# A planner that prices array forms by kind, corner products for K's tail, and six PSUM banks for attention

## The chip, the cores and the metric

The kernel runs on one core of one Trainium2 chip. The metric is the time of one execution in device microseconds. TensorE (PE) multiplies, VectorE (DVE) and ScalarE (ACT) do the elementwise work and read the results out of PSUM, SyncE (SP) issues the DMAs, and GpSimd (POOL) only sets up constants. PSUM has eight banks of 128 partitions x 512 f32.

## The reference

Two stages, one feeding the other. First linear attention over 8 batches x 8 heads, 576 tokens, head size 64, with 128 features:

```python
def phi(x):
    proj = np.einsum('bhsd,df->bhsf', x, w_phi)
    proj = proj - np.max(np.abs(proj), axis=-1, keepdims=True)
    return np.concatenate([np.exp(proj), np.exp(-proj)], axis=-1)
q_p, k_p = (phi(q), phi(k))
kv = np.einsum('bhsf,bhsd->bhfd', k_p, v)
z = np.sum(k_p, axis=2)
num = np.einsum('bhsf,bhfd->bhsd', q_p, kv)
den = np.einsum('bhsf,bhf->bhs', q_p, z)[..., None] + 1e-06
out = num / den
```

Then a gated feed-forward over the 4608 tokens (x is 4608 x 512, the inner width 1536):

```python
gate = 1.0 / (1.0 + np.exp(-(x @ w_gate)))
val = x @ w_val
y = gate * val @ w_out
```

All in f32. Attention's products run on TensorE as f32. The feed-forward's run as three fp32r products each (high x high, high x low, low x high), so each weight and each activation is held as a high and a low part (`wh`/`wl`, `xh`/`xl`, `hh`/`hl`).

## The kernel before

**Attention** goes in 32 steps, one for each batch and pair of heads. In the program's tile names a step is: `pk`, the projection of K (`keys`: eight products on 64x128 halves of the array, then one 128x128 product for the last 64 tokens of both heads, laid out in `kin` as a block diagonal, into the third bank `pk_2`); `pq`, the projection of Q in two halves of 288 tokens; `px`, a product that spreads Q's maxima (steps 0 to 9 only); `kvz`, K's features times V and their sums, in four 128x32 strips; `tp`, three 128x128 transposes of the result; `nm`, the numerator, and `dp`, the denominator, both in strips. Between them, DVE takes maxima and subtracts (`mx`, `dk`, `pm`, `mb`, `d`), and ACT takes exponentials and copies out of PSUM (`ek`, `eq`, `d`, `kvt`, `kv`, `ex`, `dr`).

**Feed-forward** takes the tokens in nine chunks of 512 and the inner width in twelve blocks j of 128. Pass A does j = 0 to 3 for all chunks while attention is still running: for each chunk and j one unit, which is 12 matmuls into a bank `gA` and 12 into a bank `vA`; ACT takes a tanh and an exponential of `gA` (`tA`, `uA`), DVE makes the gate and multiplies it with `vA` (line 812: it frees `vA`'s bank), and `hhA`/`hlA` come out. After the four units of a chunk, four `acc` groups of 12 matmuls multiply with w_out, and the half result goes to HBM (`ys`). Pass B does j = 4 to 11 in the same way with names ending in B, once the weights of these j are there. The weights have to be split into high and low parts, eight instructions for each of 36 pieces (`wraw`, `wtop`, `wmid`, `wh`, `wl`). The pieces of j = 4 to 11 are prepared after all of attention is done, since they take its SBUF.

**The order of the work** is made when the program is built. Each operation is handed to `Plan` with an engine, a cost, what it follows, the buffers it takes, a rank and (on PE) a `mode`. `Plan.run` then walks through time: of the operations that can start first it takes the lowest rank, on PE with the discount `STICK` for one of the mode that PE is already in, and 0.15 us added to the cost of one of another mode. The modes are "row" (`pk`, `pq`), "strip" (`kvz`, `nm`, `dp`) and "full" (`px`, `tp` and the whole feed-forward). The order so made is the fixed order of instructions on each engine; on the chip each engine goes through its own in order and waits for semaphores.

**PSUM banks** are handed out by the planner as well: attention after the first steps takes them from `shared` (banks 0 to 4), pass A of the feed-forward from `apart` (banks 5 to 7), pass B from all eight.

Of the kernel before, what the change touches and what calls it, by code (L numbers as in the profile page):

```python
# [19 lines left out]
B, H, S, D = 8, 8, 576, 64  # L20
F = 128
P = 128
# [11 lines left out]
JA = 4  # L34
SOON = (3,)
PERM = 10
ONPE = 10
STICK = 0.3
GATE = -1.0
EXN = 2  # L40
HN = 5
# [27 lines left out]
class Op:  # L69
    def __init__(self, eng, cost, fn, after, uses, takes, rank, mode, lag):  # L70
        self.eng, self.cost, self.fn, self.rank, self.mode = eng, cost, fn, rank, mode
        self.after, self.takes, self.lag, self.end = after, takes, lag, None
        self.left, self.then = 0, []
        for b in (*uses, *takes):
            b.users.append(self)


LAG = {"PE": 0.27, "DVE": 0.13, "ACT": 0.2, "SP": 2.0, "POOL": 0.2, None: 0.0}
# [2 lines left out]
class Plan:  # L81
# [14 lines left out]
    def run(self, trace=None):  # L96
        free, mode = collections.defaultdict(float), None
        for op in self.ops:
            op.left = len(op.after)
            for a in op.after:  # L100
                a.then.append(op)
        ready = [op for op in self.ops if not op.left]
        n = 0
        while ready:
            best = {}
            for op in ready:
                t = free[op.eng]
                for a in op.after:
                    t = max(t, a.end - (a.lag if a.eng == op.eng == "PE" else 0.0))
                op.at, taken = [], set()  # L110
                for b in op.takes:
                    u, k = b.place(taken)
                    t = max(t, u)
                    taken.add((id(b.slots), k))
                    op.at.append(k)
                if t < 1e9:
                    best.setdefault(op.eng, []).append((t, op))
            if not best:
                raise RuntimeError("no operation can start")
            eng = min(best, key=lambda e: min(t for t, _ in best[e]))  # L120
            t0 = min(t for t, _ in best[eng])

            def rank(c):
                t, op = c
                return op.rank - (STICK if op.mode and op.mode == mode else 0.0), t

            t, op = min((c for c in best[eng] if c[0] <= t0 + 0.05), key=rank)
            ready.remove(op)
            cost = op.cost
            if eng == "PE":  # L130
                cost += 0.15 if op.mode != mode else 0.0
                mode = op.mode
            if trace is not None:
                trace.append((t, cost, op))
            free[eng] = t + cost
            op.end = t + cost + op.lag
            if eng == "SP" and op.mode:
                self.wire = max(self.wire, t) + op.mode / 240.0
                op.end = max(op.end, self.wire + op.lag)
            for b, k in zip(op.takes, op.at):  # L140
                b.slots.held[k], b.n = b, k
            op.fn()
            n += 1
            for o in op.then:
                o.left -= 1
                if not o.left:
                    ready.append(o)
        assert n == len(self.ops)
# [11 lines left out]
def attention_moe(  # L160
# [10 lines left out]
    nc = tc.nc  # L171
    vec, act, pool = nc.vector, nc.scalar, nc.gpsimd
    ctx.enter_context(tc.manual_schedule())
    plan = Plan()
# [9 lines left out]
    at = right.enter_context(tc.tile_pool(name="at", bufs=2, side="right"))  # L184
    ps = ctx.enter_context(tc.tile_pool(name="ps", bufs=1, space=PSUM))
    banks = Slots(8)
    alone, shared, apart = range(8), range(5), range(5, 8)
    homes = {"wp": wp1, "ws": at}

    def bank(b, shape, name):  # L190
# [25 lines left out]
    wk = at1.tile([P, F], F32, name="wk")  # L216
# [11 lines left out]
    def head(hd):  # L228
        return slice(hd * D, hd * D + D)
# [102 lines left out]
    def attention(i):  # L332
# [22 lines left out]
        def keys():  # L355
            for g, pk in enumerate(pks):
                bank(pk, [P, 4, F], f"pk{n}_{g}")
            kx = T["kin"]
            for t in range(4):
                for hd in range(2):  # L360
                    nc.tensor.matmul(  # L361
                        pks[hd].t[:, t, :], kx[head(hd), t * P : t * P + P],
                        wk[head(hd), :], start=True, stop=True,
                    )
            nc.tensor.matmul(
                pks[2].t[:, 0, :], kx[:, 4 * P :], wk, start=True, stop=True
            )

        ko = plan("PE", 1.2, keys, [lk], [kin], pks, rank=i - 0.6, mode="row")
        mx, dk = buf("mx", 2), buf("dk", 1)  # L370
        eks = []

# [80 lines left out]
        qc = []  # L453
        for hf in range(2):
            pqs = [Buf(banks, mine) for _ in range(2)]
            qo = plan("PE", 0.6, q_half(hf, pqs), [lq, ko], [qin], pqs, rank=i - 0.5, mode="row")
            qc.append(
                plan(
                    "ACT", 2 * act_time(HS), q_copy(hf, pqs), [qo, *qc],
                    [*pqs, *([d] if hf else [])], [] if hf else [d], rank=i - 0.4,  # L460
                )
            )
# [68 lines left out]
        def kv():  # L531
# [25 lines left out]
                    )  # L557

        kvo = plan(
            "PE", 3.2 if onpe else 2.6, kv, [ke, lv, *ksum], [ek, vin, *su], [kvz],  # L560
            rank=i, mode="strip",
        )
        kvt, kvb = buf("kvt", 1), buf("kv", 2)
# [33 lines left out]
                            start=sg == 0, stop=sg == 1, tile_position=(0, o),  # L597
                        )

        no = plan("PE", 2.0, num, [qf, kd], [eq, d, kvb], nms, rank=i, mode="strip")  # L600

        def num_copy():
            T["ex"] = at.tile([P, S], F32, tag="ex", name="ex" + n, bufs=EXN)
# [6 lines left out]
        def den():  # L610
# [12 lines left out]
                        )  # L623

        do = plan(
            "PE", 1.0 + soon, den, [no], [eq, d, kvb], dps, rank=i - 0.05, mode="strip"
        )
        rb = buf("rb", 1)
        if soon:
# [136 lines left out]
                acc, a[:, ts], w[:, ws], start=first and i == 0, stop=last and i == 2  # L766
            )

    hs, hdone = {}, {}
    MM = 0.2276  # L770

    def unit(S_, C, j, rank):
        key = (S_, C)
        n = f"{S_}{C}_{j}"
        T = {}
        gb, vb = (Buf(banks, apart if S_ == "A" else alone) for _ in range(2))
        tb, ub, hb = buf("t", 1), buf("u", 2), buf("h", HN)
        hs[C, j] = hb

        def gv(m, b):  # L780
            def go():
                bank(b, [P, CW], "gv"[m] + n)
                mm_in(b.t, xs[key], j, m)

            return go

        g = plan(
            "PE", 12 * MM, gv(0, gb), [*xdone[key], *wdone[j, 0]], [xbuf[key]], [gb],
            rank=rank, mode="full",
        )  # L790
        link("unit", g)
        vo = plan(
            "PE", 12 * MM, gv(1, vb), [g, *wdone[j, 1]], [xbuf[key]], [vb],
            rank=rank, mode="full",
        )
        link("unit", vo)

        def tanh():
            T["t"] = moe.tile([P, CW], F32, tag="t", name="t" + n, bufs=1)
            act.activation(T["t"], gb.t, AF.Tanh, scale=0.5)  # L800

        def exp():
            T["u"] = moe.tile([P, CW], F32, tag="u", name="u" + n)
            act.activation(T["u"], gb.t, AF.Exp)

        def absolute():
            tu = T["t"].bitcast(U32)
            vec.tensor_scalar(tu, tu, 0x7FFFFFFF, None, op0=ALU.bitwise_and)  # L808

        def times():  # L810
            t = T["t"]
            vec.scalar_tensor_tensor(t, t, 1.0, vb.t, op0=ALU.add, op1=ALU.mult)  # L812

        def gate():
            u = T["u"]
            vec.scalar_tensor_tensor(u, u, 1.0, T["t"], op0=ALU.min, op1=ALU.mult)  # L816

        def high():
            T["h"] = tuple(
                moe.tile([P, CW], F32R, tag=x, name=x + n, bufs=HN) for x in ("hh", "hl")  # L820
            )
            hb.t = T["h"]
            act.copy(T["h"][0], T["u"])  # L823

        def rest():
            hh, hl = T["h"]
            vec.tensor_tensor(hl, T["u"], hh.bitcast(F32), op=ALU.subtract)  # L827

        r = GATE
        o = plan("ACT", act_time(CW), tanh, [g], [gb], [tb], rank=r)  # L830
        e = plan("ACT", act_time(CW), exp, [g], [gb], [ub], rank=r)
        o = plan("DVE", vec_time(CW, True), absolute, [o], [tb], rank=r)
        o = plan("DVE", vec_time(CW), times, [o, vo], [tb, vb], rank=r)
        o = plan("DVE", vec_time(CW), gate, [o, e], [tb, ub], rank=r)
        o = link("high", plan("ACT", act_time(CW), high, [o], [ub], [hb], rank=r))
        hdone[C, j] = plan("DVE", vec_time(CW), rest, [o], [ub, hb], rank=r)
        return vo
# [28 lines left out]
    for C in range(NCK):  # L866
# [5 lines left out]
        for t in range(CW // P):  # L872
# [12 lines left out]
            def store(C=C, t=t, T=T):  # L885
# [2 lines left out]
            o = plan(  # L888
                "PE", 3 * JA * MM, accumulate,
                [*(hdone[C, j] for j in range(JA)), *(w for j in range(JA) for w in wdone[j, 2])],  # L890
                [hs[C, j] for j in range(JA)], [ab], rank=100 + 10 * C + 15, mode="full",
            )
            outs.append(o)
            o = plan("ACT", act_time(DM) + 0.08, half, [o], [ab], [yb], rank=GATE)
            ydone[C].append(plan("SP", 0.06, store, [o], [yb], rank=90, mode=256))
# [9 lines left out]
    for C in range(NCK):  # L905
# [3 lines left out]
        for j in js:  # L909
# [3 lines left out]
            for t in range(CW // P):  # L913

                def accumulate(C=C, t=t, j=j, ab=accs[t], end=end):
# [4 lines left out]
                o = plan(  # L920
                    "PE", 3 * MM, accumulate,
                    [hdone[C, j], *wdone[j, 2], before[t]], [hs[C, j], *([] if j == JA else [accs[t]])],
                    [accs[t]] if j == JA else [], rank=r - 0.1, mode="full",
                )
                before[t] = o
                if not end:
# [76 lines left out]
```

## Time and profile before

| | us |
|---|---|
| median of 3 runs | 1228.23 (1225.63 to 1228.31) |
| the profiled execution | 1229.72 |
| its span, first to last instruction | 1227.8 |
| PE busy | 1204.3 (98%) |
| DVE busy | 757.1 (62%) |
| ACT busy | 517.2 (42%) |

The profiled execution is 1.5 us over the median, and 1.9 us of it lie outside the span. The granted clock over the span is 0.997. PE's busy share is counted from matmul records whose ends are modelled, and neighbouring ones overlap, so it says that PE is seldom idle and not that each instruction runs at its best rate. How long a group of matmuls holds PE is better read from the start of its first record to the start of the next group's first.

### The profile page before, as it was taken

How to read it: one execution, taken by the hardware profiler on the slowest of the kernel's cores; microseconds unless marked ns; L12 is line 12 of the kernel's file. 1: busy time of each engine (PE TensorE's matmuls, PEld its weight loads, DVE VectorE, ACT ScalarE, POOL GpSimd, SP SyncE). 2: the span in 40 equal slices, each digit the busy share in tenths (PEclk: the TensorE clock that was granted, in tenths of full speed). 3: DMA queues.
4: the chain of work that ended last, by engine and by line, in shares of the span. 5: the costliest groups of instructions: out<-in, count | busy, mean ns of one | idle time of the engine just before them, and what ended most of it. 6: DMA issues, size and time to landing. Idle time of an engine off the chain costs nothing.

```text
span 1227.8 us, 20852 instructions
## 1 busy us (share of the span) xinstructions
PE 1204.3 (98%) x8480; PEld 916.1 (75%) x8480; DVE 757.1 (62%) x1410; ACT 517.2 (42%) x1012; POOL 2.3 (0%) x11
## 2 busy tenths in 40 slices
PE   8989999999999999999999999999999999999998
PEld 6666766666666656688787888888888888888886
DVE  7989688879887789668988433434243434342333
ACT  6766566656565565643443222222222222222221
POOL 0000000000000000000000000000000000000000
PEclk9999999999999999999999999999999999999999
DMA  7786433433352524255564100102020202020100
GB/s 258 246 258 216 138 116 118 141 122 104 90 181 62 164 83 132 65 191 206 187 225 146 70 34 35 69 28 76 1 103 1 103 1 103 1 103 1 67 3 34
DMA packets 66891, 131.42 MB, mean 107 GB/s; under 512 B 16492, under 2 KB 22764, under 8 KB 64620
## 3 DMA queue, kind: packets, MB, share of 16 engines
q1 hardware_dynamic: 66796, 130.10, 32.0%
q8 instruction: 66, 1.08, 0.4%
q14 instruction: 29, 0.24, 0.1%
HBM read 92.04 MB, written 28.45 MB: 98 GB/s over the span
## 4 chain that ended last, share of the span: by engine, by line
PE 82%; DVE 10%; DMA 3%; ACT 3%; issue 2%; SPq 0%; DVEq 0%; ACTq 0%
PE acc L765 20%; PE vB L758 15%; PE gB L758 15%; PE gA L758 6%; PE vA L758 6%; PE kvz L537 5%; PE nm L595 5%; PE pq L437 3%; PE pk L361 2%; PE dp L619 2%; PE kvz L554 1%; DVE wtop L284 1%; ACT wtop L280 1%; DVE wraw L299 1%; DMA rb<-den 1%
## 5 line engine op out<-in xcount | busy, mean ns | idle before, releaser
L812 DVE SCALAR_TENSOR_TENSOR tB<-tB,vB 128x512 f32<-128x512 f32 x72 | 49.5, 687 | 200.3 <-PE vB L758 200.3
L823 ACT CAST hhB<-uB 128x512 fp32r<-128x512 f32 x72 | 44.7, 621 | 297.2 <-DVE uB L816 297.2
L765 PE MATMUL acc<-wh,hhB 128*128 128x512 f32 x288 | 112.8, 392 | 2.8 <-ACT hhB L823 2.8
L765 PE MATMUL acc<-wh,hlB 128*128 128x512 f32 x288 | 113.1, 393 | 1.2 <-DVE hlB L827 1.1
L765 PE MATMUL acc<-wl,hhB 128*128 128x512 f32 x288 | 112.7, 391 | 0.0
L758 PE MATMUL vB<-xhB,wh 128*128 128x512 f32 x288 | 112.0, 389 | 0.0
L758 PE MATMUL gB<-xhB,wh 128*128 128x512 f32 x288 | 112.0, 389 | 0.0
L758 PE MATMUL gB<-xlB,wh 128*128 128x512 f32 x288 | 112.0, 389 | 0.0
L758 PE MATMUL vB<-xlB,wh 128*128 128x512 f32 x288 | 112.0, 389 | 0.0
L758 PE MATMUL gB<-xhB,wl 128*128 128x512 f32 x288 | 112.0, 389 | 0.0
L758 PE MATMUL vB<-xhB,wl 128*128 128x512 f32 x288 | 112.0, 389 | 0.0
L800 ACT ACTIVATE tB<-gB 128x512 f32<-128x512 f32 x72 | 43.0, 598 | 122.0 <-PE gB L758 122.0
L808 DVE TENSOR_SCALAR tB<-tB 128x512 uint32<-128x512 uint32 x72 | 30.6, 426 | 97.9 <-ACT tB L800 97.9
L402 ACT ACTIVATE ek<-dk 128x512 f32<-128x512 f32 (+1 forms) x192 | 83.0, 520 | 8.9 <-DVE dk L387 8.9
L537 PE MATMUL kvz<-ek,vin 128*32 128x256 f32 x1280 | 75.5, 381 | 1.6 <-ACT d L449 1.6
L827 DVE TENSOR_TENSOR hlB<-uB,hhB 128x512 fp32r<-128x512 f32 x72 | 49.7, 691 | 41.2 <-ACT hhB L823 41.2
L765 PEld LDWEIGHTS acc<-wh,hhB 128*128 128x128 f32 x288 | 54.5, 189 | 14.8 <-ACT hhB L823 3.7
L765 PEld LDWEIGHTS acc<-wh,hlB 128*128 128x128 f32 x288 | 54.5, 189 | 13.7 <-DVE hlB L827 2.5
L765 PEld LDWEIGHTS acc<-wl,hhB 128*128 128x128 f32 x288 | 54.3, 189 | 11.4
L537 PEld LDWEIGHTS kvz<-ek,vin 128*32 128x32 f32 x1280 | 39.4, 110 | 31.3 <-issue 4.3
L758 PEld LDWEIGHTS vB<-xlB,wh 128*128 128x128 f32 x288 | 54.1, 188 | 11.3
L758 PEld LDWEIGHTS gB<-xlB,wh 128*128 128x128 f32 x288 | 54.1, 188 | 11.3
(114 smaller groups left out, 2471.4 us busy)
## 6 DMA issues: line engine op xcount, KB each, us to landing
wraw<-w_moe SPq DMA_DIRECT2D x36, 512.0 KB
kin<-k SPq DMA_DIRECT2D x32, 320.0 KB
vin<-v SPq DMA_DIRECT2D x32, 320.0 KB
qin<-q SPq DMA_DIRECT2D x32, 288.0 KB
wh<-wtop SPq DMA_DIRECT2D x36, 256.0 KB
ys<-y SPq DMA_DIRECT2D x36, 256.0 KB
xlB<-xs SPq DMA_DIRECT2D x9, 1024.0 KB
y<-ys SPq DMA_DIRECT2D x36, 256.0 KB
```

What stands on the lines that cost most here:

```text
L361: nc.tensor.matmul(pks[hd].t[:, t, :], kx[head(hd), t * P : t * P + P], wk[head(hd), :], start=True, stop=True,)
L402: act.activation(e[:, :, sg * F : sg * F + F], T["dk"][g], AF.Exp, scale=1.0 - 2.0 * sg,)
L437: nc.tensor.matmul(pqs[hd].t, wk[head(hd), :], T["qin"][head(hd), hf * HS : hf * HS + HS], start=True, stop=True,)
L537: nc.tensor.matmul(z[o : o + Q, : 2 * F], vx[:, 2 * t + hd, o % D : o % D + Q], (e0, e1)[hd][:, t, :] if t < 4 else e2[:, 0, :], start=t = ...
L595: nc.tensor.matmul(nm.t[o : o + Q, :], w[:, sg, o : o + Q], es[sg][:, o // D, cs], start=sg == 0, stop=sg == 1, tile_position=(0, o),)
L758: nc.tensor.matmul(o, a[:, ws], y[:, cs], start=i == 0, stop=i == 11)
L765: nc.tensor.matmul(acc, a[:, ts], w[:, ws], start=first and i == 0, stop=last and i == 2)
L800: act.activation(T["t"], gb.t, AF.Tanh, scale=0.5)
L808: vec.tensor_scalar(tu, tu, 0x7FFFFFFF, None, op0=ALU.bitwise_and)
L812: vec.scalar_tensor_tensor(t, t, 1.0, vb.t, op0=ALU.add, op1=ALU.mult)
L823: act.copy(T["h"][0], T["u"])
L827: vec.tensor_tensor(hl, T["u"], hh.bitcast(F32), op=ALU.subtract)
```

## The change

1. The planner has four modes where there were three: the feed-forward's products, "full" before, are now "ffn". The 0.15 us for a change of mode is replaced by a table (`turn_time`), and the time of the turn comes before the operation. `STICK` goes from 0.3 to 0.8, and an operation of the present mode may be chosen though it can start only up to `WAIT` = 0.3 us later.
2. Some PE costs in the planner are set anew (`keys` 1.2 to 1.1, `q_half` 0.6 to 0.485, `kv` 2.6 to 2.56, `num` 2.0 to 1.93, `den` 1.0 to 0.97, a feed-forward matmul 0.2276 to 0.2267).
3. Attention has six banks (0 to 5) instead of five, pass A has two (6 and 7) instead of three. Units j = 2 and 3 of a chunk's pass A may start only after the `acc` groups of the chunk before.
4. `keys`: the 128x128 product for K's last 64 tokens becomes two products on 64x64 corners of the array, head 0 on rows and columns 0 to 63, head 1 on rows and columns 64 to 127, both into `pk_2`. No operation of another engine changes.

```diff
-STICK = 0.3
+STICK = 0.8
+WAIT = 0.3
+OWN = 6
...
+LEAVE = {"ffn": 0.1, "strip": 0.1, "row": 0.2, "full": 0.1}
+
+
+def turn_time(old, new):
+
+    if old == new or old is None:
+        return 0.0
+    if (old, new) == ("full", "ffn"):
+        return 0.04
+    return LEAVE[old] + (0.11 if new == "ffn" else 0.0)
...
-            def rank(c):
-                t, op = c
-                return op.rank - (STICK if op.mode and op.mode == mode else 0.0), t
-
-            t, op = min((c for c in best[eng] if c[0] <= t0 + 0.05), key=rank)
+            if eng == "PE":
+                found = [
+                    (op.rank - (STICK if op.mode == mode else 0.0), t, op)
+                    for t, op in best[eng]
+                    if t <= t0 + 0.05 + (WAIT if op.mode == mode else 0.0)
+                ]
+                _, t, op = min(found, key=lambda c: c[:2])
+                t += turn_time(mode, op.mode)
+                mode = op.mode
...
-            if eng == "PE":
-                cost += 0.15 if op.mode != mode else 0.0
-                mode = op.mode
...
-    alone, shared, apart = range(8), range(5), range(5, 8)
+    alone, shared, apart = range(8), range(OWN), range(OWN, 8)
...
-            nc.tensor.matmul(
-                pks[2].t[:, 0, :], kx[:, 4 * P :], wk, start=True, stop=True
-            )
-
-        ko = plan("PE", 1.2, keys, [lk], [kin], pks, rank=i - 0.6, mode="row")
+            for hd in range(2):
+                nc.tensor.matmul(
+                    pks[2].t[head(hd), 0, :], kx[head(hd), 4 * P + hd * D :][:, :D],
+                    wk[head(hd), :], start=True, stop=True, tile_position=(hd * D, hd * D),
+                )
+
+        ko = plan("PE", 1.1, keys, [lk], [kin], pks, rank=i - 0.6, mode="row")
...
-    MM = 0.2276
+    MM = 0.2267
...
+        room = adone.get(C - 1) if S_ == "A" and j > 1 else None
         g = plan(
-            "PE", 12 * MM, gv(0, gb), [*xdone[key], *wdone[j, 0]], [xbuf[key]], [gb],
-            rank=rank, mode="full",
+            "PE", 12 * MM, gv(0, gb), [*xdone[key], *wdone[j, 0], room], [xbuf[key]], [gb],
+            rank=rank, mode="ffn",
         )
```

On PE 32 products are added, the second corner of each step. DVE, ACT, SP and POOL have the same instructions as before; what moves is their order.

The first place is on PE, in the second chunk of pass A. Before, first the end of unit `vA_2` with one half of `pq` behind it, then the other half:

```order
L758 MATMUL vA_2_2673<-xhA_1958,wl_742 128x512
L437 MATMUL pq_00_2694<-qin_2358,wk 128x288
L437 MATMUL pq_01_2696<-qin_2358,wk 128x288
L758 MATMUL gA_3_2699<-xhA_1958,wh_1011 128x512
...
L758 MATMUL gA_3_2699<-xhA_1958,wl_1012 128x512
L437 MATMUL pq_10_2728<-qin_2358,wk 128x288
L437 MATMUL pq_11_2730<-qin_2358,wk 128x288
L758 MATMUL vA_3_2737<-xhA_1958,wh_1011 128x512
```

And now, where a unit of the same chunk begins:

```order
L640 MATMUL dp_0_2746<-eq_2638,kv_2628 32x288 x4
L640 MATMUL dp_0_2746<-d_2336,kv_2628 32x288 x4
L596 MATMUL tp_2763<-ident,kvt_2732 128x128 x3
L458 MATMUL pq_00_2770<-qin_2485,wk 128x288
L458 MATMUL pq_01_2772<-qin_2485,wk 128x288
L458 MATMUL pq_10_2778<-qin_2485,wk 128x288
L458 MATMUL pq_11_2780<-qin_2485,wk 128x288
L779 MATMUL vA_0_2790<-xhA_2055,wh_161 128x512
```

Before, each half of a step's `pq` stands between two feed-forward groups; now both stand together behind other attention work, and the feed-forward is entered once.

The second place is on PE at the end of the keys of a step (`pk_0`, `pk_1`: the two heads' banks; `pk_2`: the last tokens), before:

```order
L361 MATMUL pk_0_2813<-wk,kin_2475 128x128
L361 MATMUL pk_1_2814<-wk,kin_2475 128x128
L365 MATMUL pk_2_2815<-wk,kin_2475 128x128
L437 MATMUL pq_00_2835<-qin_2627,wk 128x288
L437 MATMUL pq_01_2837<-qin_2627,wk 128x288
```

And now:

```order
L380 MATMUL pk_0_2820<-wk,kin_2496 128x128
L380 MATMUL pk_1_2821<-wk,kin_2496 128x128
L385 MATMUL pk_2_2822<-wk,kin_2496 64x128 x2
L458 MATMUL pq_00_2836<-qin_2623,wk 128x288
L458 MATMUL pq_01_2838<-qin_2623,wk 128x288
```

One product over all 128 output partitions has become two over 64 each.

The third place is on DVE at the start of pass B. Before, the pieces of the weights (`wtop`, `wraw`, `wl`) still stand between the instructions of the first units (`tB`, `uB`, `hlB`):

```order
L808 TENSOR_SCALAR tB_6_7706<-tB_6_7706 128x512
L284 SCALAR_TENSOR_TENSOR wtop_1_7712<-wraw_1_7650,wtop_1_7712 128x512
L295 TENSOR_SCALAR wraw_1_7650<-wraw_1_7650 128x512
L299 SCALAR_TENSOR_TENSOR wraw_1_7650<-wraw_1_7650 128x512
L304 TENSOR_SCALAR wraw_1_7650<-wtop_1_7712 128x512
L305 SCALAR_TENSOR_TENSOR wl_7612<-wraw_1_7650 128x512
L812 SCALAR_TENSOR_TENSOR tB_6_7706<-tB_6_7706,vB_6_7692 128x512
```

And now, from the end of the last piece:

```order
L324 SCALAR_TENSOR_TENSOR wl_7456<-wraw_2_7546 128x512
L834 SCALAR_TENSOR_TENSOR tB_4_7617<-tB_4_7617,vB_4_7604 128x512
L838 SCALAR_TENSOR_TENSOR uB_4_7621<-uB_4_7621,tB_4_7617 128x512
L761 TENSOR_TENSOR xlB_7593<-xlB_7593,xhB_7592 128x512 x2
L849 TENSOR_TENSOR hlB_4_7647<-uB_4_7621,hhB_4_7646 128x512
L761 TENSOR_TENSOR xlB_7593<-xlB_7593,xhB_7592 128x512 x2
L830 TENSOR_SCALAR tB_5_7756<-tB_5_7756 128x512
```

The preparation of the weights now ends ahead of the first unit of pass B (j = 4); before, eight of the 24 pieces still follow `hlB_4`.

More of the change, by code (lines that the diff above doesn't have):

```diff
@@ L121, in run @@
             t0 = min(t for t, _ in best[eng])
-            def rank(c):
-                t, op = c
-                return op.rank - (STICK if op.mode and op.mode == mode else 0.0), t
-            t, op = min((c for c in best[eng] if c[0] <= t0 + 0.05), key=rank)
+            if eng == "PE":
[7 more added lines that the diff above has]
+                mode = op.mode
+            else:
+                t, op = min(
+                    (c for c in best[eng] if c[0] <= t0 + 0.05),
+                    key=lambda c: (c[1].rank, c[0]),
+                )
             ready.remove(op)
             cost = op.cost
-            if eng == "PE":
-                cost += 0.15 if op.mode != mode else 0.0
-                mode = op.mode
             if trace is not None:
@@ L364, in keys @@
                     )
-            nc.tensor.matmul(
-                pks[2].t[:, 0, :], kx[:, 4 * P :], wk, start=True, stop=True
-            )
-        ko = plan("PE", 1.2, keys, [lk], [kin], pks, rank=i - 0.6, mode="row")
+            for hd in range(2):
+                nc.tensor.matmul(
+                    pks[2].t[head(hd), 0, :], kx[head(hd), 4 * P + hd * D :][:, :D],
+                    wk[head(hd), :], start=True, stop=True, tile_position=(hd * D, hd * D),
+                )
+        ko = plan("PE", 1.1, keys, [lk], [kin], pks, rank=i - 0.6, mode="row")
         mx, dk = buf("mx", 2), buf("dk", 1)
@@ L455, in attention @@
             pqs = [Buf(banks, mine) for _ in range(2)]
-            qo = plan("PE", 0.6, q_half(hf, pqs), [lq, ko], [qin], pqs, rank=i - 0.5, mode="row")
+            qo = plan("PE", 0.485, q_half(hf, pqs), [lq, ko], [qin], pqs, rank=i - 0.5, mode="row")
             qc.append(
@@ L559, in attention @@
         kvo = plan(
-            "PE", 3.2 if onpe else 2.6, kv, [ke, lv, *ksum], [ek, vin, *su], [kvz],
+            "PE", 3.2 if onpe else 2.56, kv, [ke, lv, *ksum], [ek, vin, *su], [kvz],
             rank=i, mode="strip",
@@ L598, in num @@
                         )
-        no = plan("PE", 2.0, num, [qf, kd], [eq, d, kvb], nms, rank=i, mode="strip")
+        no = plan("PE", 1.93, num, [qf, kd], [eq, d, kvb], nms, rank=i, mode="strip")
         def num_copy():
@@ L625, in attention @@
         do = plan(
-            "PE", 1.0 + soon, den, [no], [eq, d, kvb], dps, rank=i - 0.05, mode="strip"
+            "PE", 0.97 * (1 + soon), den, [no], [eq, d, kvb], dps, rank=i - 0.05, mode="strip"
         )
@@ L767, in mm_out @@
             )
-    hs, hdone = {}, {}
-    MM = 0.2276
+    hs, hdone, adone = {}, {}, {}
+    MM = 0.2267
     def unit(S_, C, j, rank):
@@ L793, in unit @@
             "PE", 12 * MM, gv(1, vb), [g, *wdone[j, 1]], [xbuf[key]], [vb],
-            rank=rank, mode="full",
+            rank=rank, mode="ffn",
         )
@@ L890, in attention_moe @@
                 [*(hdone[C, j] for j in range(JA)), *(w for j in range(JA) for w in wdone[j, 2])],
-                [hs[C, j] for j in range(JA)], [ab], rank=100 + 10 * C + 15, mode="full",
+                [hs[C, j] for j in range(JA)], [ab], rank=100 + 10 * C + 15, mode="ffn",
             )
+            adone[C] = o
             outs.append(o)
@@ L922, in attention_moe @@
                     [hdone[C, j], *wdone[j, 2], before[t]], [hs[C, j], *([] if j == JA else [accs[t]])],
-                    [accs[t]] if j == JA else [], rank=r - 0.1, mode="full",
+                    [accs[t]] if j == JA else [], rank=r - 0.1, mode="ffn",
                 )
```

## The prediction

> **What bounds the kernel.** I read the busy times first, then the table of stages, then PE's waits, then the timeline around single groups. The page:
>
> ```profile
> PE 1204.3 (98%) x8480; PEld 916.1 (75%) x8480; DVE 757.1 (62%) x1410; ACT 517.2 (42%) x1012; POOL 2.3 (0%) x11
> PE 82%; DVE 10%; DMA 3%; ACT 3%; issue 2%; SPq 0%; DVEq 0%; ACTq 0%
> ```
>
> PE is busy nearly always and makes up most of the chain that ended last. The stages (columns: stretch, its length, busy time of PE, PEld, DVE, ACT, POOL, clock, DMA share, GB/s):
>
> ```profile
> 0.00:80.00 80.00, 70.16 (x1060) 48.20 (x1060) 68.44 (x127) 54.90 (x116) 2.32 (x11) 0.98 0.78 256
> 80.00:520.00 440.00, 435.47 (x4353) 292.93 (x4352) 356.67 (x720) 270.58 (x559) 0.00 (x0) 1.00 0.41 127
> 520.00:640.00 120.00, 118.59 (x535) 96.69 (x524) 98.42 (x181) 52.26 (x93) 0.00 (x0) 1.00 0.56 193
> ...
> 680.00:1220.00 540.00, 537.77 (x2372) 444.74 (x2370) 200.27 (x326) 128.85 (x227) 0.00 (x0) 1.00 0.13 45
> ```
>
> Until 80 us attention runs alone, DVE is busy for 68.44 us and PE idle for 9.8: DVE is the bound. From 80 to 520 us attention and pass A share PE; from 520 to 640 pass A is alone and DVE prepares weights; after 680 pass B runs alone on a PE that has no idle time to speak of. PE's waits (who waits for whom: us in total, times, longest):
>
> ```profile
> PE pk L361 <- DMA kin<-k: 4.4, 1, 4.4
> PE dp L619 <- ACT ex L605: 2.9, 1, 2.9
> PE acc L765 <- ACT hhB L823: 2.8, 2, 2.2
> PE tp L575 <- ACT kvt L567: 2.2, 2, 1.6
> ...
> PE acc L765 <- DVE hlB L827: 1.1, 1, 1.1
> ```
>
> These five rows hold 13.4 us, of which 4.4 (the first load) and 2.2 (the last unit's `hhB`) stand at the ends, which the change leaves alone; 6.8 are left. So a gain has to come from the instructions' own time on PE, which here depends on what stood before them.
>
> **Fewer stays in the feed-forward.** A stay is a run of feed-forward groups between attention groups. Counted over the order, there are 68 before and 50 now: 18 fewer. The price of one, from the timeline (start, length of the record, engine, line, out<-in, count):
>
> ```profile
> 136.71 0.76 PE L437 MATMUL pq<-qin,wk 64*128 64x288 f32 x4
> 137.40 0.50 PE L765 MATMUL acc<-wh,hhA 128*128 128x512 f32 x1
> ...
> 140.36 0.76 PE L437 MATMUL pq<-qin,wk 64*128 64x288 f32 x4
> 141.05 0.64 PE L537 MATMUL kvz<-ek,vin 128*32 128x256 f32 x8
> ...
> 168.15 1.24 PE L437 MATMUL pq<-qin,wk 64*128 64x288 f32 x8
> 169.32 0.50 PE L758 MATMUL gA<-xhA,wh 128*128 128x512 f32 x1
> ...
> 663.39 0.39 PE L758 MATMUL vB<-xhB,wh 128*128 128x512 f32 x1
> 666.11 0.39 PE L765 MATMUL acc<-wh,hhB 128*128 128x512 f32 x1
> ```
>
> Twelve feed-forward matmuls between two halves of `pq` take 140.36 - 137.40 = 2.96 us; the same twelve in pass B take 666.11 - 663.39 = 2.72. That is 0.24 for going in and out. The halves lose as well: with the stay between them the whole takes 141.05 - 136.71 = 4.34 us, while both halves together take 169.32 - 168.15 = 1.17, so 1.17 + 2.72 = 3.89 in one piece. The price of a stay is 0.24 us at least and 0.45 at most. I take 0.38, nearer the upper end, since 12 of the 18 vanished entries come from `pq` or `pk` and 16 of the vanished exits lead there: 18 x 0.38 = 6.8 (4.3 to 8.1).
>
> Against it stand attention groups that now meet another form of the array directly. Counted without the `pk_2` groups, such changes go from 71 to 75. One costs:
>
> ```profile
> 127.87 1.06 PE L554 MATMUL kvz<-ek,ones 128*32 128x128 f32 x32
> 128.75 0.40 PE L554 MATMUL kvz<-ek,halves 128*32 128x128 f32 x8
> 129.08 1.16 PE L361 MATMUL pk<-wk,kin 64*128 64x128 f32 x16
> 130.17 0.49 PE L365 MATMUL pk<-wk,kin 128*128 128x128 f32 x2
> 130.50 0.49 PE L575 MATMUL tp<-ident,kvt 128*128 128x128 f32 x3
> ```
>
> `ones` takes 0.88 us for 32, so 0.22 for 8; `halves`, with a change of form behind it, 0.33 for 8. That is 0.11 for a change; four more, +0.4. Together **-6.4 us** (-3.9 to -7.7).
>
> **The corners.** `pk_2` took 130.50 - 130.17 = 0.33 us ahead of `tp`. Ahead of other neighbours:
>
> ```profile
> 108.38 0.49 PE L365 MATMUL pk<-wk,kin 128*128 128x128 f32 x2
> 108.62 0.48 PE L758 MATMUL gA<-xhA,wh 128*128 128x512 f32 x1
> ...
> 89.19 0.49 PE L365 MATMUL pk<-wk,kin 128*128 128x128 f32 x2
> 89.60 0.76 PE L437 MATMUL pq<-qin,wk 64*128 64x288 f32 x4
> ...
> 105.92 1.08 PE L488 MATMUL px<-pm,spread 128*128 128x36 f32 x8
> 106.83 0.53 PE L575 MATMUL tp<-ident,kvt 128*128 128x128 f32 x3
> ```
>
> 0.24 ahead of the feed-forward (4 times) and 0.41 ahead of a row or strip group (15 times); with 13 ahead of `tp` or `px` the mean is 0.36. No row of before has a 64x64 product. Each becomes two records, four in all. Nearest are the 64x128 pairs of `pk`: 16 records in 130.17 - 129.08 = 1.09, less the change behind them 0.98, so 0.12 for two that run side by side; four need 0.25, and 0.36 with a change of form behind them. Lower end: two passes at `px`'s 0.91 / 8 = 0.11 and a change, 0.33; upper end the dearest `pk_2`, 0.41. I take 0.36: **0** over 32 steps (-1.0 to +1.6). The planner's lower cost for `keys` changes nothing on the chip.
>
> Both corners write the same PSUM bank, in the same time if they run side by side; in the rows above the two heads' products of `pk` go to two banks. The Trainium skill speaks against it: "Different row tiles cannot access same PSUM bank simultaneously" (TensorEngine Tiling (Array Packing), Gotcha 1: PSUM Pressure); by that the corners would have to go one after the other, at the time that the fifth rival below gives, against 0 here. No trace here shows it. The skill's PSUM page (PSUM — Partial Sum Buffer, PSUM bank collisions raise a hardware error) lets different column tiles with disjoint partitions share a bank, which the corners are, so I give the first rule little weight.
>
> **Waits that go and come.** At the start of pass B two `acc` groups come late:
>
> ```profile
> 653.74 0.39 PE L758 MATMUL gB<-xhB,wl 128*128 128x512 f32 x1
> 654.72 0.50 PE L765 MATMUL acc<-wh,hhB 128*128 128x512 f32 x1 [0.60 <-ACT hhB L823]
> ...
> 671.78 0.39 PE L765 MATMUL acc<-wl,hhB 128*128 128x512 f32 x1
> 673.26 0.50 PE L765 MATMUL acc<-wh,hlB 128*128 128x512 f32 x1 [1.09 <-DVE hlB L827]
> ```
>
> Against 0.23 from one matmul to the next (2.72 / 12) they lose 0.75 and 1.25. On DVE a piece of weights stands ahead of the gate:
>
> ```profile
> 649.40 0.69 DVE L284 SCALAR_TENSOR_TENSOR wtop<-wraw,wtop 128x512 uint32<-128x512 uint32 x1 [0.46 <-ACT wtop L280]
> 652.38 0.68 DVE L812 SCALAR_TENSOR_TENSOR tB<-tB,vB 128x512 f32<-128x512 f32 x1
> ```
>
> In the new order the last piece ends ahead of the first `tB`, because attention, whose end starts the preparation, ends earlier. So these 2.0 us should go, and what is late next is hidden as in the rest of pass B; **-1.8** (-2.0 to 0, if the pieces themselves come late).
>
> Attention ends earlier because more of it is packed beside less feed-forward: behind the last `dp` stand 684 matmuls of pass A instead of 468, so it ends 216 x 0.227 = 49 us sooner, and 6 more by the first term: at 465 us instead of 520. DVE then has all of attention and 6.5 units of pass A fewer in that time. A unit's four instructions on DVE (the last two numbers ahead of the idle time: busy us, mean ns):
>
> ```profile
> L816 DVE SCALAR_TENSOR_TENSOR uA<-uA,tA 128x512 f32<-128x512 f32 x36 | 24.5, 681 | 1.0
> L812 DVE SCALAR_TENSOR_TENSOR tA<-tA,vA 128x512 f32<-128x512 f32 x36 | 24.4, 677 | 12.8 <-PE vA L758 12.6
> L827 DVE TENSOR_TENSOR hlA<-uA,hhA 128x512 fp32r<-128x512 f32 x36 | 24.3, 683 | 5.9 <-ACT hhA L823 5.8
> L808 DVE TENSOR_SCALAR tA<-tA 128x512 uint32<-128x512 uint32 x36 | 15.0, 415 | 6.8 <-ACT tA L800 6.7
> ```
>
> So 2.46 us a unit, 16 for 6.5, and DVE's (68.44 + 356.67) - 16 = 409 us in 465, 88% where it was 82%. Waits of PE on short links grow as DVE's free share falls. In this stage the rows above have 2.9 (`dp`, for a bank that `ex` frees) and 1.6 (`tp`); scaled by 18 / 12 they come to 6.7: +2.2. A sixth bank lengthens the links: from `kvz` to its `tp` the median work of PE in between is 2.4 us by the order, was 1.4. I take **+1.7** (-4.5, both gone, to +6). The start is DVE's in both orders: 0 (2 either way).
>
> The sum is -6.4 + 0 - 1.8 + 1.7 = **-6.5 us**. The profiled execution's 1229.72 becomes 1223.2 (span 1221.3); the median lies 1.5 under it, so 1228.2 becomes **1221.7**.
>
> **Rivals.**
> 1. Six banks take away the waits and none come: -6.4 - 2.0 - 4.5 = -12.9, so 1215.3. For it: `dp`'s wait ends with `ex`, a bank; against it: 88%. 0.15.
> 2. A 64x64 corner counts as the form of the 64x128 products: no change of form behind `pk` (32 times) nor ahead of `pk` or `pq` (12): 44 x 0.11 = 4.8 less, 1216.9. Against it: every change of tile size seen in these rows costs. 0.10.
> 3. DVE becomes the bound of the whole attention stage. In the first 80 us, where it is one, it reaches 68.44 / 80 = 86%; at that share its 409 us need 476, 11 more than 465, and 9 more than I counted: 1231. Against it: it can be fuller if its work is there in time. 0.13.
> 4. **Slower**: pass A on two banks. A `vA` group needs the bank that line 812 of the unit before frees; the `gA` group between leaves 2.72 us, line 812 takes 0.68, so 2.0 are spare. A piece of weights in its way takes 652.38 - 649.40 = 2.98, so PE waits 0.94. Eighteen units follow attention now; if all are hit, 17 us, 1239. It decides from 0.57 a unit on (6.5 + 3.7 = 10.2 over 18). Against it: in pass B the same pieces cost PE two waits in eight units. 0.08.
> 5. The corners one after the other: four passes of 0.11 and a change, 0.55, 0.19 more than 0.36, 32 times: +6.1, 1227.8. 0.06.
>
> **How the numbers follow.** My own sum has 0.48, with a range of 1217 to 1226. About 0.3% (3.7 us) is what a measurement of this kernel can tell from no change: faster is under 1224.5, slower over 1231.9. Faster: 0.41 of my 0.48, rivals 1 and 2, 0.66. Same: 0.07, half of rival 3, rival 5 and a little: 0.22. Slower: rival 4 and the rest of 3: 0.12. The range of 1213 to 1230 leaves out rival 4, the longer half of 3 and the far tail of 1, under 0.2.
>
> **What would show it.** In the profile after: a `pk_2` group of 0.33 to 0.41 us; stays of 2.96 as before, fewer of them; the last `dp` near 465 us; DVE at 88% up to there; no wait on `hhB` or `hlB` but the last; PE's waits between 80 and 465 us at 4 to 8. Wrong: `vA` or `acc` groups that wait for line 812 (rival 4), or waits on DVE all through attention (rival 3).

## The result and the profile after

| | before | after |
|---|---|---|
| median, us | 1228.27 (1225.63 to 1229.43) | 1217.0 (1216.63 to 1218.63) |
| the profiled execution, us | 1229.72 | 1216.63 |
| its span, us | 1227.8 | 1214.8 |

The ratio is 0.9914, with a 95% interval of 0.9896 to 0.9932: 11.3 us faster between the medians, 13.0 between the spans. The forecast was 1221.7, from 1213 to 1230. The direction and the range held; the gain is nearly twice the 6.5 us of the sum.

The page of the kernel after, first the engines' busy times, then the chain that ended last:

```profile
PE 1201.1 (99%) x8544; PEld 916.2 (75%) x8544; DVE 755.7 (62%) x1410; ACT 516.4 (43%) x1012; POOL 2.3 (0%) x11
PE 85%; DVE 10%; ACT 2%; issue 2%; DMA 1%; SPq 0%; DVEq 0%; ACTq 0%
```

PE has the 64 records of the second corners more and is busy 3 us less. The stages (stretch, length, busy time of PE, PEld, DVE, ACT, POOL, clock, DMA share, GB/s):

```profile
0.00:80.00 80.00, 73.71 (x1040) 51.84 (x1041) 68.51 (x126) 54.26 (x114) 2.31 (x11) 1.00 0.77 252
80.00:465.00 385.00, 384.14 (x4252) 254.50 (x4252) 340.34 (x696) 257.25 (x537) 0.00 (x0) 1.00 0.46 141
60.00:80.00 20.00, 18.72 (x215) 12.85 (x214) 18.69 (x35) 12.78 (x30) 0.00 (x0) 1.00 0.78 265
```

And two rows of before that the prediction doesn't show:

```profile
80.00:465.00 385.00, 380.47 (x3823) 256.27 (x3819) 313.78 (x635) 236.22 (x489) 0.00 (x0) 1.00 0.42 132
60.00:80.00 20.00, 16.32 (x287) 10.79 (x276) 19.19 (x37) 12.76 (x30) 0.00 (x0) 1.00 0.81 255
```

In the first 80 us PE is idle for 6.3 us, where it was 9.8, on the same DVE work (68.5 us in both), and the clock is 1.00 instead of 0.98. Most of that lies between 60 and 80 us, where PE was idle for 3.7 us and now is for 1.3. From 80 to 465 us DVE is busy for 340.34 / 385 = 88%, as forecast, and yet PE is idle for only 0.86 us; in the same stretch of before it was 4.5.

PE's waits (who waits for whom: us in total, times, longest), the whole list:

```profile
PE pk L380 <- DMA kin<-k: 4.1, 1, 4.1
PE acc L786 <- ACT hhB L845: 2.2, 1, 2.2
PE kvz L558 <- ACT ex L626: 0.9, 1, 0.9
PE pk L380 <- ACT d L470: 0.8, 1, 0.8
PE pq L458 <- DVE dk L408: 0.8, 1, 0.8
PE gA L779 <- DVE xlA L730: 0.5, 1, 0.5
PE gA L779 <- ACT y L905: 0.4, 2, 0.2
PE kvz L575 <- issue: 0.2, 1, 0.2
PE acc L786 <- ACT y L905: 0.2, 1, 0.2
```

Together 10.1 us, where the list of before adds up to 19.4. The first load and the last unit's `hhB` stay, as said; `dp`'s 2.9, `tp`'s 2.2 and the `hlB` wait are gone, and nothing of their size has come.

Single groups on PE in the timeline (start, length of the record, engine, line, out<-in, form, count):

```profile
123.31 0.50 PE L779 MATMUL gA<-xhA,wh 128*128 128x512 f32 x1
...
126.27 0.69 PE L616 MATMUL nm<-eq,kv 128*32 128x288 f32 x8
...
130.41 0.43 PE L385 MATMUL pk<-wk,kin 64*64 64x128 f32 x4
130.77 0.76 PE L458 MATMUL pq<-qin,wk 64*128 64x288 f32 x4
...
140.18 0.44 PE L385 MATMUL pk<-wk,kin 64*64 64x128 f32 x4
140.55 0.55 PE L596 MATMUL tp<-ident,kvt 128*128 128x128 f32 x3
...
459.08 0.67 PE L640 MATMUL dp<-d,kv 128*32 128x288 f32 x8
```

A stay of twelve matmuls takes 126.27 - 123.31 = 2.96 us, the same as before. The corners take 0.36 and 0.37 us ahead of two different neighbours. The last `dp` runs at 459 us; the forecast was 465.

**Own time and lost time.** Waits and spans don't add up by themselves (waits -9.3, spans -13.0), since a change of form can lie inside a wait and a low clock is no wait. So I split PE's time in another way: for each matmul, the median spacing to the next one of the same pair (same operations, place in the group and neighbouring form) over the twelve profiles of this study is its own time, and what it took beyond that is lost, be it a wait or the clock. Worked out from the traces, in us from the start of PE's first matmul to the start of its last group of twelve, which leaves out the first load and the last group itself:

| kernel | total | own | lost | lost 0-465 | lost 465-680 |
|---|---|---|---|---|---|
| before | 1214.9 | 1195.5 | 19.4 | 12.9 | 4.8 |
| after | 1202.2 | 1190.0 | 12.2 | 6.8 | 3.9 |
| before with corners | 1214.3 | 1196.5 | 17.8 | 13.0 | 3.2 |
| after without corners | 1201.2 | 1189.4 | 11.8 | 6.2 | 3.9 |
| after, five banks | 1207.9 | 1192.4 | 15.5 | 14.1 | -0.2 |
| before, six banks | 1228.7 | 1192.7 | 36.1 | 7.5 | 27.0 |
| the same, with the rule for units 2 and 3 | 1206.8 | 1193.4 | 13.3 | 8.5 | 2.9 |
| after without that rule | 1223.4 | 1189.4 | 34.0 | 7.8 | 24.7 |
| after without corners, more DVE work | 1228.6 | 1188.6 | 40.0 | 32.9 | 5.5 |

Before to after: own time -5.5, lost time -7.2. The first answers to the forecast's -6.4 for the forms and 0 for the corners; the second was forecast at -0.1. The totals are read from the traces as they are, their split depends on the pairs: with the pairs told apart a little more or less finely, the own time of the change comes out between -4.6 and -7.2 and the lost time between -8.1 and -5.5. So differences of less than about 1.5 us in these two columns say little. The rows below the second are the experiments.

### The profile page after: what moved, and what is told of

It is laid out like the page before. It is cut to its first block, busy times and chain, and to the rows that moved or that the text cites. A ratio compares the mean times of both kernels' runs of the same rounds, so it can differ in the third digit from the quotient of the medians.

```text
span 1214.8 us, 20971 instructions
## 1 busy us (share of the span) xinstructions
PE 1201.1 (99%) x8544; PEld 916.2 (75%) x8544; DVE 755.7 (62%) x1410; ACT 516.4 (43%) x1012; POOL 2.3 (0%) x11
## 4 chain that ended last, share of the span: by engine, by line
PE 85%; DVE 10%; ACT 2%; issue 2%; DMA 1%; SPq 0%; DVEq 0%; ACTq 0%
PE acc L786 21%; PE vB L779 16%; PE gB L779 16%; PE kvz L558 6%; PE nm L616 5%; PE gA L779 5%; PE vA L779 5%; PE pq L458 3%; PE pk L380 2%; PE dp L640 2%; PE kvz L575 2%; DVE wtop L303 1%; DVE wraw L318 1%; PE tp L596 1%; ACT wtop L299 1%
## 5 line engine op out<-in xcount | busy, mean ns | idle before, releaser
L786 PEld LDWEIGHTS acc<-wh,hlB 128*128 128x128 f32 x288 | 54.5, 189 | 11.7 <-DVE hlB L849 0.4
L779 PEld LDWEIGHTS vB<-xhB,wh 128*128 128x128 f32 x288 | 54.1, 188 | 11.3
L779 PEld LDWEIGHTS gB<-xlB,wh 128*128 128x128 f32 x288 | 54.1, 188 | 11.2
```

What stands on the lines that cost most here:

```text
L779: nc.tensor.matmul(o, a[:, ws], y[:, cs], start=i == 0, stop=i == 11)
L786: nc.tensor.matmul(acc, a[:, ts], w[:, ws], start=first and i == 0, stop=last and i == 2)
```

## The experiments

**1. The corners alone**, in the order of before:

```diff
-            nc.tensor.matmul(
-                pks[2].t[:, 0, :], kx[:, 4 * P :], wk, start=True, stop=True
-            )
+            for hd in range(2):
+                nc.tensor.matmul(
+                    pks[2].t[head(hd), 0, :], kx[head(hd), 4 * P + hd * D :][:, :D],
+                    wk[head(hd), :], start=True, stop=True, tile_position=(hd * D, hd * D),
+                )
```

> The kernel before with the two 64x64 corners in place of the 128x128 product and nothing else; the order of all other instructions is that of before. My sum: nothing, 0 us within -1.0 to +1.6. If a 64x64 corner counted as the form of the 64x128 products, -4.8 us; if the two corners ran one after the other, +6.1 us. In the trace a pk_2 group, from its first start to the next group's, should take about 0.37 us ahead of every neighbour.

Measured: 1228.52 us, ratio 1.000 (0.999 to 1.001), span 1226.9. The corners bring nothing by themselves, as expected. This run has the order of before, and its lost time of the first 465 us is the same (13.0), but it lies elsewhere: the clock of the first 80 us was 0.94 and PE idle from 80 to 465 us 1.2 us instead of 4.5. `dp`'s wait for `ex` is 1.2 us here and was 2.9. So the single wait rows of before are not fixed by the order.

**2. All but the corners**: the kernel after with one 128x128 product for K's tail (the diff above, turned round), same order.

> The changed kernel with the 128x128 product for K's last tokens put back; the order of everything else is that of the changed kernel. If the corners are worth nothing, this takes the changed kernel's time, 1217.0 within 1.6 us. If they bring a part of the 11 us, it is slower by that part: by 4.8 if they count as the form of the 64x128 products.

Measured: 1214.43 us, ratio 0.9895 (0.9879 to 0.9911), span 1212.4: 2.6 us under the kernel after, where 1.6 at most were expected. In the own time the corners explain 0.6 of that at most. The rest was suspected in the end of the program, where the last matmuls had different clocks, so both kernels ran again, side by side.

> The kernel after, run again beside the one with one 128x128 product in place of the corners. Both theories: its median comes within 1 us of 1217.0.

> The kernel after with one 128x128 product for K's last tokens, in the same order, run again beside the kernel after. Theory 1 (the corners cost nothing, and the 2.6 us of the first comparison were the clock of the last matmuls): the two medians lie within 1 us of each other. Theory 2 (the corners cost time by their neighbours, about 0.05 us for each of the 32): this one is 1.5 to 3 us faster again.

Measured: 1215.65 us with the corners (ratio 0.9898, 0.9881 to 0.9915), 1215.01 without (0.9890, 0.9874 to 0.9907). The kernel with corners is 1.35 us under its first median, a little more than the 1 us expected. The difference between the two is 0.6 us, within what can be told from none. The end of the program in the first run of the kernel after:

```profile
1206.29 0.50 PE L786 MATMUL acc<-wh,hhB 128*128 128x512 f32 x1 [2.23 <-ACT hhB L845]
...
1207.58 0.62 PE L786 MATMUL acc<-wl,hhB 128*128 128x512 f32 x1
...
1210.56 0.59 PE L786 MATMUL acc<-wh,hlB 128*128 128x512 f32 x1
```

and in the second run of the same kernel:

```profile
1206.86 0.50 PE L786 MATMUL acc<-wh,hhB 128*128 128x512 f32 x1 [2.22 <-ACT hhB L845]
...
1208.15 0.40 PE L786 MATMUL acc<-wl,hhB 128*128 128x512 f32 x1
...
1209.78 0.40 PE L786 MATMUL acc<-wh,hlB 128*128 128x512 f32 x1
```

Behind the same wait of 2.2 us the last twelve matmuls take 4.27 us from the first start to the last in one run and 2.92 in the other. In the first run the granted clock (third column from the right) falls to a half there:

```profile
1204.16:1207.57 3.41, 1.28 (x4) 0.78 (x5) 2.04 (x4) 0.62 (x1) 0.00 (x0) 1.00 0.00 0
1207.57:1210.98 3.41, 3.41 (x9) 2.31 (x7) 2.05 (x3) 0.00 (x0) 0.00 (x0) 0.50 0.40 154
```

In the second run it stays at 1.00 to the last matmul. That 1.35 us comes and goes with the run, not with the kernel.

**3. The new prices and the corners, with five banks**: 62 stays instead of 50.

```diff
-OWN = 6
+OWN = 5
```

> The changed kernel with five banks for attention and three for pass A, as before: the planner's prices, its four modes, the corners and the rule on units 2 and 3 stay. The order has 62 stays in the feed-forward (68 before, 50 in the changed kernel) and 540 pass A matmuls behind the last dp. Theory 1, the gain is the stays and their price is 0.38 us: 6 fewer than before, about -2.3 us, so 1226, and PE's waits as before. Theory 2, the planner's prices also order the work so that waits go: -2.3 and up to -6 of waits, 1220. Theory 3, the banks are what takes the waits away: waits of PE of 15 us or more stay here.

Measured: 1223.23 us, ratio 0.9962 (0.9949 to 0.9976). PE's longest waits:

```profile
PE pk L380 <- DMA kin<-k: 4.0, 1, 4.0
PE acc L786 <- ACT hhB L845: 2.2, 1, 2.2
PE pq L458 <- ACT d L470: 2.2, 3, 0.9
PE pk L380 <- issue: 1.6, 1, 1.6
```

None of the three theories is met: the time lies between the first two, and the sign of the third, waits of 15 us or more, did not come. The whole list adds up to 11.2 us, nearly as little as with six banks (10.1), and `dp`'s and `tp`'s rows are gone without a sixth bank. Yet the lost time in the first 465 us is 14.1 us, no less than before, and about a third of it is the clock:

```profile
70.25:73.67 3.42, 1.73 (x13) 1.20 (x11) 3.42 (x9) 2.36 (x6) 0.00 (x0) 1.00 1.02 376
73.67:83.91 10.24, 9.32 (x38) 6.34 (x39) 9.62 (x14) 6.04 (x12) 0.00 (x0) 0.50 1.04 334
```

PE is idle for half of 3.42 us, and for the next 10.24 us it gets half the clock, which costs it up to 5.1 us (an estimate: half of 10.24). This is not one unlucky execution: the clock over the span was 0.993 to 0.995 in all six, against 0.998 to 1.000 in the eight of the kernel after. What the prices did bring with five banks is own time (-3.1, with only 6 stays fewer) and the start of pass B (4.8 to -0.2). The drop in the first 465 us did not come without the sixth bank.

**4. Six banks alone**, with the old prices and modes, 52 stays:

```diff
-    alone, shared, apart = range(8), range(5), range(5, 8)
+    alone, shared, apart = range(8), range(6), range(6, 8)
```

> The kernel before with six banks for attention and two for pass A and nothing else: three modes, the flat 0.15 us, the old costs, the 128x128 product. The order has 52 stays and 648 pass A matmuls behind the last dp. Theory 1, stays at 0.38 us: 16 fewer, -6 us. Theory 3, banks also take the waits away: PE's waits fall from 19.4 us to near the 10 of the changed kernel and the time to 1213 to 1219, no worse than the changed kernel by more than 2. Theory 2, waits go by the planner's prices: 1222 and waits of 15 us or more. If two banks for pass A cost anything, vA groups wait for line 812.

Measured: 1244.57 us, ratio 1.0137 (1.0120 to 1.0155): 16 us slower, which none of the theories had. Two stages of the table:

```profile
80.00:465.00 385.00, 384.65 (x4179) 256.69 (x4177) 341.63 (x696) 254.19 (x533) 0.00 (x0) 1.00 0.45 138
465.00:680.00 215.00, 195.84 (x860) 154.43 (x861) 139.27 (x251) 78.04 (x136) 0.00 (x0) 0.98 0.43 148
```

PE's two largest waits:

```profile
PE acc L765 <- ACT y L883: 8.1, 11, 0.9
PE acc L765 <- DVE tA L812: 7.4, 3, 4.0
```

From 80 to 465 us PE is idle for 0.35 us. Behind attention it is idle for 19.2 us. The timeline shows how:

```profile
501.34 0.68 DVE L812 SCALAR_TENSOR_TENSOR tA<-tA,vA 128x512 f32<-128x512 f32 x1
502.07 0.50 PE L765 MATMUL acc<-wh,hhA 128*128 128x512 f32 x1 [0.88 <-DVE tA L812]
...
505.28 0.58 ACT L883 ACTIVATE y<-acc 128x512 f32<-128x512 f32 x1
505.91 0.50 PE L765 MATMUL acc<-wh,hhA 128*128 128x512 f32 x1 [0.80 <-ACT y L883]
```

The first `acc` waits for line 812, which frees `vA_3`'s bank, and each later `acc` for the copy `y` of the one just before it. The order on PE behind attention, group by group (twelve matmuls each), is

```
gA_3 vA_3 acc_0 acc_1 acc_2 acc_3 gA_0 vA_0 gA_1 vA_1 gA_2 vA_2 gA_3 vA_3 acc_0 ...
```

**5. The same, with the rule of the change** that units 2 and 3 of a chunk wait for the `acc` groups of the chunk before:

```diff
+        room = adone.get(C - 1) if S_ == "A" and j > 1 else None
...
-            "PE", 12 * MM, gv(0, gb), [*xdone[key], *wdone[j, 0]], [xbuf[key]], [gb],
+            "PE", 12 * MM, gv(0, gb), [*xdone[key], *wdone[j, 0], room], [xbuf[key]], [gb],
```

> The kernel before with six banks for attention, two for pass A, and the rule that units 2 and 3 of a chunk wait for the acc groups of the chunk before; the planner's three modes, flat 0.15 us, old costs and the 128x128 product stay. The order has 53 stays and, behind attention, two units of the next chunk between vA_3 and the acc groups. Theory 1: the rule is what makes two banks bearable; the 19 us that PE lost behind attention with six banks alone go, and the time is 1215 to 1220 (15 stays fewer at 0.38, waits as in the changed kernel). Theory 2: the planner's prices are needed for it; 1232 or more, with acc still waiting for line 812 and for the copy y.

Measured: 1221.47 us, ratio 0.9943 (0.9924 to 0.9962), 23 us less than experiment 4 and 1.5 over the first theory's range. The order is now

```
gA_3 vA_3 gA_0 vA_0 gA_1 vA_1 acc_0 acc_1 acc_2 acc_3 gA_2 vA_2 gA_3 vA_3 ...
```

The stage behind attention, in the columns of the table of stages:

```profile
465.00:680.00 215.00, 214.07 (x971) 173.55 (x970) 147.84 (x268) 80.69 (x143) 0.00 (x0) 1.00 0.45 148
```

PE is idle for 0.9 us of this stretch. The rule reads as a limit, but what it does is to let two units of the next chunk in ahead of `acc_0`, so that the last gate of the chunk is ready and its bank free by then.

Side by side with experiment 3 this splits the change in two. The sixth bank with its rule, under the old prices, brings 7.9 us against the kernel before that ran beside it; the prices and the corners, with the rule but five banks, bring 5.0. Both together bring 11.3, and 12.9 in the second run: the two parts nearly add up.

**6. The change without the rule**, the test from the other side (in the line above, `room = None`):

> The changed kernel without the rule on units 2 and 3. The order has 51 stays (50 with it), and behind attention the acc groups stand straight behind vA_3. Theory 1 (the rule holds off the two banks' price): about 4 us lost for each chunk behind attention, 15 to 20 us in all, so 1232 to 1237, with acc groups waiting for line 834 and for the copy y. Theory 2 (the planner's prices do it): 1217 within 2.

Measured: 1237.81 us, ratio 1.0069 (1.0047 to 1.0092), 20.8 us over the kernel after, about as the first theory has it. The same stage:

```profile
465.00:680.00 215.00, 197.17 (x837) 156.37 (x836) 141.13 (x254) 77.73 (x135) 0.00 (x0) 0.99 0.42 145
```

The idle time is back in the same place (17.8 us), with the same two waits on `y` and on the gate (8.6 and 5.8 us).

**7. More work on DVE**, to see at which share the waits come: from the kernel without corners, the subtraction of the first group of keys is done three times instead of once (64 more instructions, which write the same values again).

```diff
-                vec.tensor_tensor(
-                    dkt, pks[g].t[:, :ns, :],
...
+                for _ in range(3 if g == 0 else 1):
+                    vec.tensor_tensor(
+                        dkt, pks[g].t[:, :ns, :],
```

> The changed kernel with the 128x128 product put back (1214.4), and the first 128x512 subtraction of each step's K made three times instead of once, the same values again: 64 more DVE instructions of 0.68 us, about 0.6 each in a row, 38 us in all, 9 of them in the first 75 us where DVE is the bound. The order of all else is kept. DVE's share between 80 and 465 us goes from 88% to 96% or more. Theory 1, waits grow as DVE's free share falls (my term): from 12% free to 4%, three times the waits; with the start's 9 us, PE loses 10 us or more between 80 and 465 and the time is 1235 or more. Theory 2, with six banks the work stands far enough ahead and PE waits only once DVE's work no longer fits: the start's 9 us, 2 to 4 us later, 1224 to 1228.

Measured: 1243.3 us, ratio 1.0118 (1.0099 to 1.0136), 28.9 us over experiment 2, in the first theory's range of 1235 or more. The stage from 80 to 465 us:

```profile
80.00:465.00 385.00, 371.76 (x3962) 248.63 (x3966) 363.94 (x727) 246.44 (x513) 0.00 (x0) 1.00 0.46 142
```

Three of PE's largest waits:

```profile
PE pk L380 <- DVE dk L407: 5.7, 5, 2.2
PE pq L457 <- DVE dk L407: 4.4, 2, 2.8
PE tp L595 <- ACT kvt L587: 3.5, 3, 1.8
```

DVE's share came to 363.94 / 385 = 94.5%, not to the 96% expected. PE is idle for 13.2 us of this stretch, at 88.4% (the kernel after) for 0.86. The free share fell to about a half and the idle time grew fifteenfold, so the waits don't grow in proportion; nothing between 88% and 94.5% was measured. The added instructions also stand on the path from `pk` to `ek` themselves, so part of this is the longer link and not the share; the two weren't separated.

**8. One bank more**: seven for attention, one for pass A, without corners; 43 stays.

```diff
-OWN = 6
+OWN = 7
```

> The changed kernel with the 128x128 product put back and seven banks for attention, one for pass A. The order has 43 stays and 780 pass A matmuls behind the last dp. Each vA group then needs the bank that ACT reads for tanh and exponential, and each gA group the one that line 832 frees. Theory 1, banks of pass A are the price: some 2 us a unit behind attention, 20 units, 30 us or more slower than the changed kernel, 1250 or more. Theory 2, fewer stays outweigh it: 1212.

Measured: 1300.28 us, ratio 1.0582 (1.0560 to 1.0604). PE's two largest waits:

```profile
PE vA L777 <- ACT uA L824: 24.3, 21, 1.6
PE gA L777 <- DVE tA L832: 14.7, 16, 1.7
```

The stage behind attention:

```profile
465.00:680.00 215.00, 161.84 (x636) 116.52 (x636) 125.67 (x226) 64.63 (x110) 0.00 (x0) 0.99 0.37 128
```

Every `vA` now needs the bank of the `gA` just before it. The own time falls once more (to 1184.5 us), and the lost time grows by some 90 us. Of the three splits of eight banks that ran under the new prices, six and two is the best.

## Why the prediction was right, and what it missed

**What bounds.** PE, before and after: the gain is own time of PE plus time that PE lost.

**Fewer stays, -6.4.** Measured as own time: -5.5, or -6.1 where the corners are left out (1195.5 to 1189.4). The size is right and the account behind it is coarser than it looked: six banks alone save 16 stays and 2.8 us of own time (0.18 a stay), the prices with five banks save 6 stays and 3.1 us. Part of that is the prediction's second item, changes of form between attention groups, 71 before: they are 83 with six banks alone, 71 with five banks and the new prices, 75 after. With both of its prices the sum would be -4.8 for the first and -2.3 for the second, so the price of a stay isn't one number, and which groups stand at its sides counts too. That the mean of 0.34 over the 18 came near my 0.38 for this order is in part luck. Which of the new prices (`STICK`, `WAIT`, the table of turns, the costs) brings what was not tried.

**The corners, 0.** 0.36 to 0.37 us a group, as taken, ahead of every neighbour (one of the 32, in the first step, took 0.62), and at that 11.7 us for the 32 groups of the kernel after, the same as the 128x128 products take in its order. They run side by side: in each of the 32 groups the two corners start 6 to 7 ns apart, and the second pair of records 0.16 us or more behind the first. Rival 5 would have needed 0.55 a group. Rival 2 (no change of form at their sides) would have needed about 0.25 and is out too. The rule of the Trainium skill that the prediction gave little weight (TensorEngine Tiling (Array Packing), Gotcha 1: PSUM Pressure) does not hold here: two corners on different rows, with disjoint output partitions, wrote one bank within one 0.37 us group of four records. The ground for the little weight was poor, though: right behind the sentence that the prediction used, the PSUM page of the Trainium skill (PSUM — Partial Sum Buffer, PSUM bank collisions raise a hardware error) says the same of row tiles as the rule does. The step came out right by the trace, not by the page.

**Waits that go and come, -1.8 + 1.7.** This is the step that failed. Its first half held in kind: the `hlB` wait and one of the two `hhB` waits are gone, and the lost time from 465 to 680 us fell by 0.9, half of what was forecast. The failing step is "scaled by 18 / 12 they come to 6.7: +2.2", on the ground that "Waits of PE on short links grow as DVE's free share falls". DVE's share came out as forecast (88%), and from 80 to 465 us PE's idle time fell from 4.5 to 0.86 us where it was to rise. The rows that were scaled, `dp`'s 2.9 and `tp`'s 1.6, were taken as a property of the order, and they are not: the same order left PE idle for 1.2 us there in experiment 1. Nor is it shown that a sixth bank is what takes `dp`'s wait away, though `dp` waited for a bank: with five banks and the new prices (experiment 3) the row is gone too, and PE is idle for 0.92 us.

What the runs do show is the sum. Lost time in the first 465 us is 13 to 14 us in the three kernels with five banks and 6 to 8.5 in the five with six (that with more DVE work left out). With five it differs in kind: in before one stretch of 3.41 us at half clock lies in it, in experiment 1 three, in experiment 3 the one of 10.24 us. What these three share is PE's idle time from 60 to 80 us, 3.1 to 3.7 us against 1.2 to 2.1 with six banks, and a late first feed-forward product, at 79.8 to 84.0 us against 73.8 to 76.8. So with six banks the work that fills PE comes earlier. Why the planner's order does that was not followed up.

**The start, 0 (2 either way).** This term failed as well: PE's idle time there fell by 3.5 us, more than the 2 allowed, and the clock rose from 0.98 to 1.00. "DVE's in both orders" was true of DVE's 68.5 us, not of what PE could do meanwhile. Of the 6.1 us of lost time that went in the first 465 us, between 1 and 3 lie here, by how the pairs are told apart.

**The rivals.** Rival 1, six banks take away waits and none come, gave 1215.3 and had 0.15, near the 1217.0 and 1215.65 measured. (Rival 2's 1216.9 is as near by luck: its mechanism is refuted above.) The account of rival 1 is half right: no new waits came, but what went lies partly in the first 80 us and in the clock, which it didn't name. The prediction itself wrote its term down as an end of the range (-4.5, both gone). Rival 3, DVE as the bound, is refuted at 88%. Rival 4, pass A on two banks, is a real price, and a larger one than worked out: 21 to 23 us without the rule (experiments 4 to 6). It was put on `vA` groups that wait for line 812; it falls on `acc` groups, which wait for line 812 and for each other's copies. That it stays away is the work of the rule, whose effect the prediction didn't price.

## What to carry to other kernels

Don't scale a single row of a wait list before the same order has run once more: here `dp`'s 2.9 us was 1.2 in another run of the same order. An engine's busy share alone says little of the waits on it: at 88% of DVE PE was next to never idle. When a pool gives a buffer away, look for the place where the poorer side runs alone, and put independent work between the last writer and the first reader there: here one rule decided between 1.4% slower and 0.6% faster. And compare lost time, waits and clock together, since a low clock can stand where a wait stood.

## What the runs showed of the chip

The granted clock of the first 80 us differed from run to run of the kernels and went with PE's idle time in that stretch: 1.00 in the five profiles with 6.2 to 6.7 us idle, 0.94 to 0.98 in the seven with 7.9 to 10.5 (before, for one, 9.8 and 0.98; with the corners alone 9.6 and 0.94). The traces have an order for the two. Where the granted clock is under 1.00, it is 0.50 for 3.41 us or, twice, for 10.24 us at a stretch. There are 24 such stretches ahead of PE's last matmul in the twelve profiles, and each stands right behind 3.41 us in which PE was busy for 0.48 to 2.62 us, as in the rows of experiments 2 and 3. The idle time comes first, then the low clock. Not every idle stretch brings it: in the second run of the kernel after PE was busy for 1.18 us from 1204.20 to 1207.60, and the clock stayed at 1.00. What decides was not tried.

After a 2.2 us wait, seven of the last twelve matmuls of one and the same kernel ran at 0.43 us each in one execution (1207.58 to 1210.56) and at 0.23 in another.

A 64x64 product counts as a form of its own, since its group would take 0.25 us without a change of form by the prediction's estimate: it costs 0.37 us ahead of each neighbour, where the 128x128 product cost 0.24 ahead of the feed-forward, 0.33 ahead of `tp` and 0.41 ahead of a row or strip group.
